# Full-height score matmuls against a zero-padded q, padded by SBUF-to-SBUF DMAs, in a kernel of sparse attention and a two-layer network

## The chip, the cores and the metric

The kernel runs on one core of a Trainium2 chip. The metric is the device time of one execution in microseconds (us), median of several; lower is better. A run comes with the clock granted to TensorE, as a share of full speed. PE is TensorE's matmuls, PEld its weight loads, DVE is VectorE, ACT is ScalarE, POOL is GpSimd, SP is SyncE (which only issues transfers here); SPq and POOLq are their queues of issues. A transfer *lands* when its data have arrived and a waiting engine may go on. A *stop* or *hole* is a time in which TensorE stands still. A *drain* is the time that TensorE takes to empty itself when the number of rows in use changes. PSUM is the memory that TensorE writes its results to. Each run has a state: *slow* if its time is over 1.5% above the fastest of the same kernel, else *fast*.

## The reference

```python
# attention: batch 8, 8 heads, 576 positions, head size 64
scores = scale * (q @ k^T)
local   = (rel >= 0) & (rel < 32)                       # heads 0 to 3
strided = (rel >= 0) & (pos_k % 32 == pos_q % 32)       # heads 4 to 7
out = softmax(masked scores) @ v
# network on the 4608 tokens: 512 -> 2048 -> 512
h = x @ w_in
g = max(h, 0) + alpha * min(h, 0)
y = g @ w_out
```

The inputs q and k are drawn at 0.1 of unit size, so all scores are near zero.

## The kernel before

The network is cut into 9 chunks of 512 tokens; pieces of attention are woven between the pieces of its two layers, so that TensorE always has a dense matmul to do. Heads go in pairs: `g = 4*batch + pair`, pairs 0 and 1 local, 2 and 3 strided. q and k of a pair stand transposed on 128 partitions, one head (or, for strided pairs from batch 3 on, one of two positions) on rows 0 to 63, the other on rows 64 to 127. A score group multiplies each half on its own:

```python
# score_piece: groups of 3 tiles of 96 queries (local) or 4 tiles of 72 (strided)
for x, t in enumerate(grp):
    ...
    for y in range(2):
        hf = slice(64 * y, 64 * y + 64)
        matmul(sps[y][:, w*x : w*x + w], P.kT[hf, k0 : k0 + 128],
               P.qT[hf, q0 : q0 + w], ...)          # 64 rows, two halves side by side
```

From batch 3 on (`DX = 3`) the strided q and k are transposed by DMA, not by TensorE:

```python
def load_d(b):            # GpSimd: q, k of batch b, heads 4..7 -> qks
def transpose_d():        # SyncE: qks -> qT1, kT1 by DMA transpose, q first
```

What is issued where, in the weave of pair g (c is its batch; cuts marked by ...):

```python
okT = 8 <= t < npair and (t % 4 == 0 or t < 4*DX and t % 2 == 0)     # t = g + 1: local transposes
seq: S (scores 0), P (PV 0), T (transpose q), X, S2 (scores 1), P, Tk (transpose k), P
todo = casts of v                       if g % 4 == 0
todo = casts of the next local q and k, each followed by the load of the one after   if g % 4 == 1
...
if lastp:                                # after the last P of the pair
    if g % 4 == 0 and DX <= c < B: transpose_d()
    if g % 4 == 2 and DX <= c and c + 1 < B: load_d(c + 1)
    if g % 4 == 2 and c + 2 < B:             load_v(c + 2, False)
```

The softmax here doesn't subtract the row's maximum and nothing guards it: scores larger than these inputs give would overflow.

Of the kernel before, what the change touches and what calls it, by code (L numbers as in the profile page):

```python
# [10 lines left out]
F16 = mybir.dt.float16  # L11
# [20 lines left out]
def kernel(  # L32
# [10 lines left out]
    nc = tc.nc  # L43
    keep = tc.keep_in_program_order

    B, H, S, D = q.shape
# [7 lines left out]
    cpool = ctx.enter_context(tc.tile_pool(name="const", bufs=1))  # L54
# [15 lines left out]
            name=nc.get_next_instruction_name(), act_func_set_id=6, ins=[], outs=[]  # L70
# [8 lines left out]
    mfirst, mother, mstr = consts[:, 128:416], consts[:, 224:320], consts[0:72, 416:488]  # L79
# [7 lines left out]
    DX = 3  # L87
    qTs = [cpool.tile([128, 2, 672], F16, name=f"qT{i}") for i in range(2)]
# [2 lines left out]
    vss = [cpool.tile([128, 4, 8, 65], F16, name=f"vs{i}") for i in range(2)]  # L91
    ets = [cpool.tile([128, 640], F16, name=f"et{i}") for i in range(NE)]
    x16s = cpool.tile([80, 1024], F16)
    qks = {nm: cpool.tile([80, 4, 512], F16, name=f"{nm}sd") for nm in "qk"}


# [27 lines left out]
    def transpose_d():  # L124

        for nm, dst in (("q", qTs[1]), ("k", kTs[1])):
            o = dst.rearrange("r e c -> r (e c)")[:, 0:1280].rearrange("r (j p) -> r j p", p=80)
            keep(nc.sync.dma_start_transpose(o, qks[nm].rearrange("p h c -> p (h c)")))

    def cast_s(b, nm, eng):  # L130
        t16 = hpool.tile([128, 2, 512], F16, tag=f"{nm}s", bufs=3, name=f"{nm}s")
# [8 lines left out]
    def load_tail(b, strided):  # L140

        t16 = tpool.tile([128, 512], F16, tag="tl", name="tl16")
        for i, src in enumerate((q, k)):
            if strided:
                keep(nc.gpsimd.dma_start(
                    t16[32 * i : 32 * i + 32, :].rearrange("x (h c) -> x h c", h=4),
                    src[b, 4:8, 512:576, :].rearrange("h (x c) d -> x h (c d)", c=2)))
            else:
                keep(nc.gpsimd.dma_start(
                    t16[64 * i : 64 * i + 64, 0:256].rearrange("p (h d) -> p h d", h=4),  # L150
                    src[b, 0:4, 512:576, :].rearrange("h p d -> p h d")))
        cast16[(b, strided, "tail")] = t16
# [122 lines left out]
    def score_piece(P, i):  # L275

        et = ets[ectr["i"] % NE]
        if wide["on"] and ectr["i"] % 2:
            sps = [phpool.tile([128, 512], F32, tag="hps", name="sph") for _ in range(2)]
        else:  # L280
            sp = pbpool.tile([128, 2, 512], F32, tag="sp", name="sp")
            sps = [sp[:, y] for y in range(2)]
        ectr["i"] += 1
        w, grp = P.w, P.sgroups[i]
        n = w * len(grp)
        r = 72 if P.strided else 128
        early = P.b < NEARLY
        for x, t in enumerate(grp):
            if P.dx:
                q0 = k0 = 80 * (4 * (2 * P.pr + t % 2) + t // 2)  # L290
            else:
                q0, k0 = w * t, 32 + 72 * t if P.strided else 96 * t
            for y in range(2):
                hf = slice(64 * y, 64 * y + 64)
                keep(nc.tensor.matmul(  # L295
                    sps[y][:, w * x : w * x + w], P.kT[hf, k0 : k0 + 128],
                    P.qT[hf, q0 : q0 + w], start=(x == 0),
                    stop=(x == len(grp) - 1 and not early), skip_group_check=True))

                key = (2 * (t // 2) + y, t % 2) if P.strided else (t, y)  # L300
                P.et[key] = (et, n * y + w * x)
        first = not P.strided and i == 0
        if early:

            if first:
                m = madd[:, 0:288]
            else:
                m = madd[0:72, 288:360] if P.strided else madd[:, 96:192]
                m = m.unsqueeze(1).to_broadcast([r, n // w, w])
            for y in range(2):  # L310
                keep(nc.tensor.matmul(  # L311
                    sps[y][:, 0:n], ident[0:r, :], m, start=False, stop=True, skip_group_check=True))
        ev = et[0:r, 0 : 2 * n]
        if wide["on"] and ectr["i"] % 2 == 0:
            for y in range(2):
                keep(nc.scalar.activation(
                    ev[:, n * y : n * y + n], sps[y][0:r, 0:n], AF.Exp, scale=SCALE))
        else:
            keep(nc.scalar.activation(  # L319
                ev.rearrange("r (y c) -> r y c", y=2), sp[0:r, :, 0:n], AF.Exp, scale=SCALE))  # L320
        if early:
            return
        if first:
            ev = ev.rearrange("r (y c) -> r y c", y=2)
            m = mfirst.unsqueeze(1).to_broadcast([r, 2, n])
        else:
            ev = ev.rearrange("r (c f) -> r c f", f=w)
            m = (mstr if P.strided else mother).unsqueeze(1).to_broadcast([r, 2 * n // w, w])
        keep(nc.gpsimd.tensor_tensor(ev, ev, m, op=ALU.mult))  # L329
# [57 lines left out]
    npair = 4 * B  # L387
# [61 lines left out]
    for g in range(7, npair + 2):  # L449
        c = g // 4  # L450
        a, p, t = g, g - 1, g + 1
        okA = 8 <= a < npair
        okP = 8 <= p < npair
        okT = 8 <= t < npair and (t % 4 == 0 or t < 4 * DX and t % 2 == 0)
        nP = len(pairs[p].pgroups) if okP else 0
        seq = []
        if okA:
            seq.append(("S", Sc(a, 0)))
        if okP:
            seq.append(("P", Pv(p, 0)))  # L460
        if okT:
            seq.append(("T", T(t // 2, "q")))
        if 8 <= g - 2 < npair and not pairs[g - 2].xd:
            seq.append(("X", X(g - 2)))
        if okA:
            seq.append(("S2", Sc(a, 1)))
        if okP:
            seq.append(("P", Pv(p, 1)))
        if okT:
            seq.append(("Tk", T(t // 2, "k")))  # L470
        if nP == 3:
            seq.append(("P", Pv(p, 2)))
        if not seq:
            seq.append(("N", lambda: None))

        todo = [(c, pr) for pr in range(2)] if g % 4 == 0 and 8 <= g < npair else []

        if g % 4 == 1 and 9 <= g and c + 1 < B:
            todo = [(c + 1, nm) for nm in "qk"]
        lastP = max([i for i, z in enumerate(seq) if z[0] == "P"], default=len(seq) - 1)  # L480
        copyP = next((i for i, z in enumerate(seq) if z[0] == "S2"), 0)
        nslots = [i for i, z in enumerate(seq) if z[0][0] != "S"] or list(range(len(seq)))
        for i, (kind, fn) in enumerate(seq):
            extra = []
            if todo and i in nslots:
                left = len([z for z in nslots if z >= i])
                cnt = -(-len(todo) // max(1, left))
                extra = [todo.pop(0) for _ in range(min(cnt, len(todo)))]

            def run(fn=fn, extra=extra, g=g, c=c, kind=kind, lastp=(i == lastP), copyp=(i == copyP)):  # L490
                fn()
                for b, pr in extra:
                    if pr in ("q", "k"):
                        cast_l(b, pr)
                        if b + 1 < B:
                            load_qk(b + 1, False, pr)
                        continue
                    cast_v(b, pr, "pool")
                    if pr == 1 and b + 1 < B:
                        load_v(b + 1, True)  # L500
                if kind == "Tk" and g % 4 == 3 and c + 3 < B:
                    load_tail(c + 3, False)
                if lastp:
                    if 4 * DX <= g - 1 < npair and pairs[g - 1].xd:
                        x_dma(pairs[g - 1])
                    if g % 4 == 0 and DX <= c < B:
                        transpose_d()
                    if g % 4 == 2 and DX <= c and c + 1 < B:
                        load_d(c + 1)
                    if g % 4 == 2 and c + 2 < B:  # L510
                        load_v(c + 2, False)
                if copyp and 4 * DX <= g - 2 < npair and pairs[g - 2].xd and pairs[g - 2].strided:
                    x_copy(pairs[g - 2])
            feed(run, g - 2 if kind == "X" else -1)
# [98 lines left out]
    def load_unit(b, strided, v_too=True):  # L613
        load_qk(b, strided, "q")
        load_qk(b, strided, "k")
        load_tail(b, strided)
        if v_too:
            load_v(b, strided)
# [83 lines left out]
    while pos["i"] < end1:  # L702
        attn_step(end1)
    wide["on"] = False
    load_unit(3, False)
    load_d(3)

# [48 lines left out]
```

## Time and profile before

| what | before |
|---|---|
| median, range | 334.2 us, 334.1 to 334.5 |
| span in the profile | 332.4 us |
| PE, DVE, ACT, POOL busy | 96%, 56%, 52%, 43% |
| granted clock | 1.00 |

The prediction shows the page and timeline lines. One line more of the kernel before, from the table of stretches: stretch, its length, then busy us of PE, PEld, DVE, ACT and POOL (with counts), granted clock, DMA share and GB/s.

```profile
118.00:152.00 34.00, 33.61 (x268) 16.14 (x266) 19.69 (x39) 19.42 (x32) 18.96 (x18) 1.00 1.03 135
```

In the 34 us of one batch TensorE is busy 33.6 us at full clock. Where costs are worked out below, one dense matmul of 512 columns counts 0.2157 us from start to start, as in the prediction (0.216 is the median of the trace).

### The profile page before, as it was taken

How to read it: one execution, taken by the hardware profiler on the slowest of the kernel's cores; microseconds unless marked ns; L12 is line 12 of the kernel's file. 1: busy time of each engine (PE TensorE's matmuls, PEld its weight loads, DVE VectorE, ACT ScalarE, POOL GpSimd, SP SyncE). 2: the span in 40 equal slices, each digit the busy share in tenths (PEclk: the TensorE clock that was granted, in tenths of full speed). 3: DMA queues.
4: the chain of work that ended last, by engine and by line, in shares of the span. 5: the costliest groups of instructions: out<-in, count | busy, mean ns of one | idle time of the engine just before them, and what ended most of it. 6: DMA issues, size and time to landing. Idle time of an engine off the chain costs nothing.

```text
span 332.4 us, 6351 instructions
## 1 busy us (share of the span) xinstructions
PE 320.5 (96%) x2533; PEld 163.2 (49%) x2533; DVE 185.1 (56%) x363; ACT 172.5 (52%) x300; POOL 142.2 (43%) x154
## 2 busy tenths in 40 slices
PE   6899999999999999999999999999999999999995
PEld 2554455554554444444558754445444444444444
DVE  5477836477553873387428833784368337605800
ACT  2644753467535744575457644773476336425611
POOL 7932497137679365736483528332611400000000
PEclk9999999999999999999999999999999999999999
DMA  6999999399398649683979295715530120011011
GB/s 220 191 207 207 236 210 194 85 245 157 66 87 125 200 59 147 114 234 40 154 138 221 25 153 109 133 13 109 129 67 20 49 85 33 0 65 63 0 63 65
DMA packets 73117, 39.22 MB, mean 118 GB/s; under 512 B 54064, under 2 KB 64768, under 8 KB 73088
## 3 DMA queue, kind: packets, MB, share of 16 engines
q0 software_dynamic: 41760, 17.38, 48.7%
q1 hardware_dynamic: 31328, 21.44, 26.0%
q8 instruction: 20, 0.33, 0.4%
q14 instruction: 9, 0.07, 0.1%
HBM read 38.01 MB, written 9.44 MB: 143 GB/s over the span
## 4 chain that ended last, share of the span: by engine, by line
PE 89%; DVE 4%; ACT 3%; DMA 2%; issue 1%; SPq 0%; ACTq 0%
PE ops L586 37%; PE hps L544 36%; PE pv L345 4%; PE sp L295 4%; PE tp L235 3%; DMA ql<-in_q_dram 2%; DVE x L354 1%; PE wps L608 1%; PE ops L577 1%; ACT xT L366 1%; DVE qT L177 1%; ACT osb L591 1%; PE sp L311 1%; PE sph L311 1%; PE xp L362 1%
## 5 line engine op out<-in xcount | busy, mean ns | idle before, releaser
L586 PE MATMUL ops<-wout,gT 128*128 128x512 f16 x560 | 136.9, 379 | 0.2 <-DVE gT L557 0.2
L544 PE MATMUL hps<-xT,win 128*128 128x512 f16 (+1 forms) x640 | 134.3, 358 | 2.5 <-ACT xT L366 2.0
L557 DVE SCALAR_TENSOR_TENSOR gT<-neg,oma,hps 128x512 f16<-128x512 f32 x144 | 106.0, 744 | 49.8 <-ACT neg L554 42.2
L554 ACT ACTIVATE neg<-hps 128x512 f32<-128x512 f32 x144 | 86.0, 597 | 46.4 <-PE hps L544 45.2
L329 POOL TENSOR_TENSOR et<-et,consts 128x576 f16<-128x576 f16 (+1 forms) x48 | 61.1, 1274 | 95.4 <-ACT et L319 95.3
L544 PEld LDWEIGHTS <-win 128*128 128x128 f16 x640 | 59.4, 98 | 59.4 <-issue 6.1
L586 PEld LDWEIGHTS <-gT 128*128 128x128 f16 x560 | 48.3, 97 | 46.3 <-issue 0.5
L319 ACT ACTIVATE et<-sp 72x576 f16<-72x576 f32 (+1 forms) x56 | 36.1, 645 | 29.2 <-PE sp L295 15.3
L591 ACT COPY osb<-ops 128x512 f32<-128x512 f32 x35 | 20.5, 585 | 53.4 <-PE ops L586 49.6
L352 DVE RECIPROCAL rc<-pv 72x6 f32<-72x6 f32 (+2 forms) x80 | 14.9, 186 | 55.7 <-PE pv L345 55.6
L354 DVE TENSOR_TENSOR x<-pv,rc 96x384 f16<-96x384 f32 (+2 forms) x65 | 34.5, 531 | 2.2
L345 PEld LDWEIGHTS <-et 72*128 72x128 f16 (+1 forms) x448 | 23.4, 98 | 16.5 <-DVE x L354 1.1
L295 PEld LDWEIGHTS <-kT 64*128 64x128 f16 x448 | 10.8, 95 | 26.5 <-issue 21.2
L295 PE MATMUL sp<-qT,kT 64*128 64x72 f16 (+1 forms) x392 | 16.9, 201 | 1.9 <-ACT kT L175 1.7
L177 DVE COPY qT<-tp 128x1024 f16<-128x1024 f16 (+1 forms) x11 | 11.3, 1030 | 12.3 <-PE tp L235 12.3
L608 PE MATMUL wps<-wrm 128*128 128x512 f16 x44 | 15.7, 428 | 1.2 <-DVE wrm L620 1.2
L167 POOL DMA_DIRECT2D vl<-in_v_dram x8 | 11.1, 1394 | 10.7 <-PE xp L362 9.1
L345 PE MATMUL pv<-vs,et 72*128 72x65 f16 x256 | 15.3, 194 | 0.1
L179 POOL COPY vs<-stv 72x1024 f16<-72x1024 f16 x14 | 14.3, 1032 | 0.0
L175 ACT COPY kT<-tp 128x1024 f16<-128x1024 f16 (+1 forms) x11 | 9.4, 858 | 8.4 <-PE tp L235 8.4
L345 PE MATMUL pv<-vl,et 128*128 128x65 f16 x192 | 11.1, 194 | 0.0
L383 ACT COPY xT<-xs 128x576 f16<-128x576 f16 x5 | 6.5, 1301 | 5.2 <-DMA xs<-x16s 5.2
(73 smaller groups left out, 169.5 us busy)
## 6 DMA issues: line engine op xcount, KB each, us to landing
out_dram<-osb SPq DMA_DIRECT2D x35, 256.0 KB, 2.3
ql<-in_q_dram SPq DMA_DIRECT2D x6, 512.0 KB, 5.5
kl<-in_k_dram SPq DMA_DIRECT2D x6, 512.0 KB, 6.6
stv<-in_v_dram POOLq DMA_DIRECT2D x8, 288.0 KB, 6.2
vl<-in_v_dram POOLq DMA_DIRECT2D x6, 384.0 KB, 9.8
win<-in_moe_w_in_dram POOLq DMA_DIRECT2D x4, 512.0 KB, 10.1
wout<-in_moe_w_out_dram POOLq DMA_DIRECT2D x4, 512.0 KB, 17.1
ql<-in_q_dram POOLq DMA_DIRECT2D x3, 512.0 KB, 8.9
```

The costliest lines, as they stand in the source:

```text
L295: keep(nc.tensor.matmul(sps[y][:, w * x : w * x + w], P.kT[hf, k0 : k0 + 128], P.qT[hf, q0 : q0 + w], start=(x == 0), stop=(x == len(grp) ...
L319: keep(nc.scalar.activation(ev.rearrange("r (y c) -> r y c", y=2), sp[0:r, :, 0:n], AF.Exp, scale=SCALE))
L329: keep(nc.gpsimd.tensor_tensor(ev, ev, m, op=ALU.mult))
L345: keep(nc.tensor.matmul(pv[:, 65 * x : 65 * x + 65], et[0:r, c : c + 128], v16[0:r, 2 * P.pr + hh, t, :] if P.strided else v16[:, 6 * (2 * ...
L352: keep(nc.vector.reciprocal(rc[0:w, 0:nb], pvv[:, :, 64]))
L354: keep(nc.vector.tensor_tensor(P.x16[0:w, c0 : c0 + 64 * nb].rearrange("r (c e) -> r c e", e=64), pvv[:, :, 0:64], rc[0:w, 0:nb].unsqueeze ...
L544: keep(nc.tensor.matmul(hps[:, dst : dst + w], win16[:, kk, 128 * m : 128 * m + 128], xT[:, kk, src : src + w], start=(kk == 0 and x == 0) ...
L554: keep(nc.scalar.activation(neg, hps, AF.Relu, scale=-1.0))
L557: keep(nc.vector.scalar_tensor_tensor(gTs[n][:, m, :], neg, oma[:, m : m + 1], hps, op0=ALU.mult, op1=ALU.add))
L586: keep(nc.tensor.matmul(ops, gTs[n][:, kf, 128 * mt : 128 * mt + 128], wout16[:, kf, :], start=(kf == 0), stop=(kf == 15)))
L591: keep(nc.scalar.copy(osb, ops))
L608: keep(nc.tensor.matmul(wps, wrm[:, 0:128], wrm, start=True, stop=True))
```

## The change

The intent: each tile's two halves become one full-height matmul. A padded copy `qz` holds two blocks of q for each tile, the first with rows 64 to 127 zero, the second with rows 0 to 63 zero. One block of keys (128 rows) then serves a moving operand of `2w` columns. TensorE streams twice the columns, but the 64-row mode is left. The padded copies are made by DMA from `qT`; their zeros are written once, by GpSimd before batch 3. To give the copies time, the local transposes go one pair earlier (with the small loads that follow them), and the casts and loads of q and k change places with the casts of v and the load of the strided v that follows them.

```diff
+    qzs = [cpool.tile([128, 2, 1280 if i else 1152], F16, name=f"qz{i}") for i in range(2)]
+    mloc = cpool.tile([128, 576], F16)
...
+    def pad_q(u):                                  # two DMAs of 64 partitions on SyncE
+        src = qTs[u % 2].rearrange("r e c -> r (e c)") if u % 2 else qTs[0][:, :, 0:576]
+        for y in range(2):
+            hf = slice(64 * y, 64 * y + 64)
+            if u % 2:
+                keep(nc.sync.dma_start(qzs[1][hf, y, :], src[hf, 0:1280]))
+            else:
+                keep(nc.sync.dma_start(
+                    qzs[0][hf, y, :].rearrange("r (e c) -> r e c", e=2), src[hf]))
...
+            if P.b >= DX:
...
+                qz = qzs[1 if P.strided else 0]
+                c = 2 * w * x
+                cuts = [(0, 2)] if c // n == (c + 2 * w - 1) // n else [(0, 1), (1, 2)]
+                for y0, y1 in cuts:
+                    bk, o = divmod(c + w * y0, n)
+                    keep(nc.tensor.matmul(
+                        sps[bk][:, o : o + w * (y1 - y0)], P.kT[:, k0 : k0 + 128],
+                        qz[:, y0:y1, q0 : q0 + w], ...))
...
-        okT = 8 <= t < npair and (t % 4 == 0 or t < 4 * DX and t % 2 == 0)
+        okT = 8 <= t < 4 * DX and t % 2 == 0
+        if 4 * DX <= g + 2 < npair and g % 4 == 2:
+            okT, t = True, g + 2
...
-        todo = [(c, pr) for pr in range(2)] if g % 4 == 0 and 8 <= g < npair else []
-        if g % 4 == 1 and 9 <= g and c + 1 < B:
+        todo = [(c, pr) for pr in range(2)] if g % 4 == 1 and 8 <= g < npair else []
+        if g % 4 == 0 and 8 <= g and c + 1 < B:
             todo = [(c + 1, nm) for nm in "qk"]
...
+                if kind == "Tk" and t >= 4 * DX:
+                    pad_q(t // 2)
...
                     if g % 4 == 0 and DX <= c < B:
                         transpose_d()
+                        pad_q(1)
```

## The prediction

> **What bounds the kernel now.** I read the page's busy table and slices first, then the table of stretches, the PE timeline of one batch, and last the DMA issues around the point where the change puts a new transfer.
>
> The busy table and the two slice rows of the kernel before:
>
> ```profile
> PE 320.5 (96%) x2533; PEld 163.2 (49%) x2533; DVE 185.1 (56%) x363; ACT 172.5 (52%) x300; POOL 142.2 (43%) x154
> ...
> PE   6899999999999999999999999999999999999995
> ...
> PEclk9999999999999999999999999999999999999999
> ```
>
> TensorE is busy from end to end at the full granted clock and nobody else passes 56%. So what counts is TensorE time: work on it, or waits of it. Busy time alone hides short stalls (matmul records overlap), so I read start times. The PE timeline of one batch that the change touches (start, length of the merged group, operation, count):
>
> ```profile
> 203.37 1.03 PE L586 MATMUL ops<-wout,gT 128*128 128x512 f16 x4
> 204.33 0.30 PE L295 MATMUL sp<-qT,kT 64*128 64x96 f16 x6
> 204.56 1.04 PE L586 MATMUL ops<-wout,gT 128*128 128x512 f16 x4
> 205.44 0.35 PE L345 MATMUL pv<-vl,et 128*128 128x65 f16 x6
> 205.62 1.03 PE L586 MATMUL ops<-wout,gT 128*128 128x512 f16 x4
> 206.48 0.42 PE L362 MATMUL xp<-consts,x 72*128 72x72 f16 x8
> 206.74 0.81 PE L544 MATMUL hps<-xT,win 128*128 128x512 f16 x3
> 207.91 2.10 PE L544 MATMUL hps<-xT,win 128*128 128x512 f16 x9 [0.35 <-ACT xT L366]
> ...
> 212.09 1.89 PE L544 MATMUL hps<-xT,win 128*128 128x512 f16 x8
> 213.92 0.30 PE L295 MATMUL sp<-qT,kT 64*128 64x72 f16 x8
> 214.15 1.90 PE L544 MATMUL hps<-xT,win 128*128 128x512 f16 x8
> ```
>
> Four dense matmuls of 512 columns take 206.48 - 205.62 = 0.86 us start to start, 0.2155 each: 512 columns at 0.417 ns plus some 2.5 ns. Eight transposes of 72 columns take 0.26 us and six PV matmuls of 65 take 0.18: the same rate, with no loss when they begin or end. The score groups (L295, 64 rows) alone lose time: four dense from 203.37 should have handed over at 204.23, and the score starts at 204.33, **0.10 us later**; and after it another hole before 204.56.
>
> **What the Trainium skill says.** "TensorEngine Tiling (Array Packing)", Key Properties: "Changing tiling mode (not just tile) drains the TensorE". The trace agrees in its sign and gives the size: some 0.1 us going into a 64-row group and the like coming out, and none between groups of 72, 96 and 128 rows, which are evidently one mode. "TensorE: Matmul & The Clock Gate", Back-to-back issue gap, gives N/2.4 + 2.5 ns warm; the 0.2155 us above agrees (213.3 + 2.5 = 215.8). The same page's row on small-K matmuls says that two 64-row halves run concurrently; the change gives that up. "DMA: Bandwidth & Descriptors", anatomy of one DMA, gives about 2 us fixed per transfer (stated for the GpSimd path) and says that a wait is held by the issuing sequencer; here a 256 KB store from SyncE lands in 2.3 us (DMA issues on the page).
>
> **The change, part by part.**
>
> *Score matmuls.* Per batch there are 4 pairs of 2 score groups. Batches 3 to 7 make 40 groups, 20 local and 20 strided. Now, cost of a group = start of the dense run after it minus start of the dense run before it minus the dense matmuls:
> local 204.56 - 203.37 - 4 x 0.2157 = 0.327 us; strided 214.15 - 212.09 - 8 x 0.2157 = 0.334 us.
> After: each tile's two halves become one moving operand of 2w columns against one full-height block of keys. A local group of 3 tiles has 6 x 96 = 576 columns; its middle tile crosses the bank edge and is cut in two, so 4 matmuls. A strided group has 4 matmuls of 144, also 576 columns. Both: 576/2.4 + 4 x 2.5 = 0.250 us. The array streams **twice** the columns, but without the two drains. Saving 20 x 0.077 + 20 x 0.084 = **3.2 us**, 1.0% of the run. All of it lies on TensorE, the bound, so it should show in full. The count of score matmuls falls from 280 to 160 in these batches, all matmuls from 2533 to 2413 or so. Weight loads are at most 128 columns, some 98 ns each but hidden (PV does one each 30 ns), so they stay hidden.
>
> *Masks and exp.* Same 576 columns; the masks read a stored 128x576 pattern instead of a broadcast for the first local group. Zero in effect: 1.27 us each on POOL, which has slack.
>
> *Setup.* Four memsets and six small copies on POOL, queued after the casts that end near 56 us, where POOL then idles 9.1 us until 65.2 and again 7.3 us before 76.6. A 32-column memset took 0.33 us; even some 2.5 us for each of the long ones (my estimate by size, generous) would fit. Zero.
>
> *Order.* The local transposes move one pair earlier (same batch), the casts of q and k change places with those of v. The same pieces are in each chunk. The wait of 0.5 us at 207.91 (ACT copies xT after the output copy) is of a part that does not move; I expect it to stay.
>
> *The pads.* Per batch four SBUF-to-SBUF transfers of 64 partitions, 147 or 164 KB each, 0.6 MB a batch, some 18 GB/s beside the 102 to 135 GB/s in the table of stretches. Volume is harmless. **Latency is the question**: for the strided pairs the pad can be issued only after the DMA transpose of q has landed, and the scores then wait for pad, not transpose. DMA issues of batch 4 (135 us on), median us to landing:
>
> ```profile
> stv<-in_v_dram POOLq DMA_DIRECT2D x1, 288.0 KB, 6.0
> qT<-qsd SPq DMA_TRANSPOSE x1, 7.5
> kT<-ksd SPq DMA_TRANSPOSE x1, 7.2
> ```
>
> and SyncE's and PE's timelines there:
>
> ```profile
> 135.72 1.34 SPq L128 DMA_TRANSPOSE qT<-qsd  x1
> 137.15 4.35 SPq L128 DMA_TRANSPOSE kT<-ksd  x1
> ...
> 145.76 0.30 PE L295 MATMUL sp<-qT,kT 64*128 64x72 f16 x8
> ```
>
> q is there at 135.7 + 7.5 = 143.2, k at 144.35, the strided scores at 145.76: a margin of 2.5 us for q. Two pads need two issues of 0.33 us (as a store's) and 2.3 us to land: about 2.9 us. So 0.4 us short here. By the same subtraction for the other batches (issue of the transpose, its landing, start of the strided scores): batch 3 100.7 + 5.9 against 111.7, margin 5.1; batch 5 169.3 + 6.5 against 179.8, 3.9; batch 6 203.4 + 7.4 against 213.9, 3.0; batch 7 237.5 + 3.8 against 250.8, 9.4. Two things move these: in batches 3 to 5 the 1 MB of loads of the next q and k, now issued after the transposes, come **ahead** of them, with the second on SyncE right before (some 0.6 us of issue, and its bytes in front); and the 288 KB load of v, which today runs beside the transposes, comes a step later. Batch 7, which has neither, shows the transpose alone at 3.8 us. I take these two as about even, up to 2 us worse in batches 3 to 5 and better in batch 6. That gives a stall of 1 to 2 us in batch 4, up to 1 in batch 5, none in 3, 6, 7.
> The local pads come from engine transposes issued a whole pair ahead (that is what the earlier order buys), over 7 us before use: at the edge when they share the queues with the v loads (a transpose of x issued there took 7.6 us), so I allow some tenths.
>
> Sum: -3.2 (scores) + about 1.0 (waits for pads) = -2.2 us: 334.2 - 2.2 = **332.0 us**.
>
> **The rivals.** (a) *Pads fully hidden*: 331.0 us. For: the transpose lands early if v's load no longer competes. (b) *The pad becomes the new wait*: SyncE holds its queue until q has landed and the strided scores of each batch stop TensorE by 1 to 3 us, 3 to 10 us in all: 333 to 341. For: margins of 2.5 to 3.9 us against a need of 2.9. Against: only three batches have the loads in front. (c) *Doubled columns cost more than thought*, with a two-part moving operand read slower or full-height weights not loaded ahead: at 90 ns a matmul a group costs 0.36 us and the change loses 1 us. Against: PV and transposes, full height with weights of their own each, run at column rate. (d) *SyncE held back delays the output stores* until the 3 output buffers run out. Against: the last store of a chunk falls there, and the next is some 9 us off, so no stall.
>
> **Range and chances.** (a) is the low end, 330.4 with some tenths for waits that vanish as well; (b) in its middle is the high end, 335.5. Faster by over 2% needs under 327.6, twice the whole gain: 0.02. Slower by over 2% needs 341, all of (b): 0.03. Within: 0.95.
>
> **What would show it.** The score groups at L313 should have 128 rows, 160 of them, and take 0.25 us between dense runs without the 0.1 us holes. TensorE's wait lists should show a pad landing, if at all, before the first strided scores of batches 4 and 5. PEclk must stay at 9. I am wrong if the holes stay at full height, if the matmuls of 144 and 192 columns run slower than their columns, or if the strided scores wait over 2 us for a pad in several batches.

## The result, and the profile after

The changed kernel takes **359.1 us** (355.9 to 359.8) against 334.2. Its ratio to before is 1.072, with a 95% interval of 1.067 to 1.078. Ratios here are the mean time of one kernel's fast runs over that of the other's fast runs of the same rounds, so they are not quite the ratio of the medians. The profiled run is one of 355.9 us.

The page of the kernel after, busy table and two slice rows:

```profile
PE 323.9 (91%) x2413; PEld 171.1 (48%) x2413; DVE 184.5 (52%) x363; ACT 173.6 (49%) x300; POOL 148.3 (42%) x164
...
PE   7899999999999967989597995999899998999995
...
PEclk9999999999999996999989998999999999999999
```

The matmuls fell from 2533 to 2413 as intended, but the PE row now has gaps in the middle, and the clock row has a 6 and some 8s where it had only 9s. The same stretch as shown of before, in the kernel after:

```profile
118.00:152.00 34.00, 28.50 (x200) 14.62 (x197) 13.45 (x30) 15.29 (x25) 17.74 (x17) 0.90 0.99 141
```

TensorE is busy 5 us less here, and at a mean clock of 0.90. Its timeline in that stretch (start, length of the merged group, operation, form, count, idle time before it and what ended it):

```profile
122.27 1.89 PE L622 MATMUL ops<-wout,gT 128*128 128x512 f16 x8
123.99 0.41 PE L313 MATMUL sp<-qz,kT 128*128 128x144 f16 x4
124.24 1.03 PE L622 MATMUL ops<-wout,gT 128*128 128x512 f16 x4
...
128.44 1.03 PE L622 MATMUL ops<-wout,gT 128*128 128x512 f16 x4
134.62 0.64 PE L313 MATMUL sp<-qz,kT 128*128 128x192 f16 x4 [5.15 <-DMA qz<-qT]
135.05 1.91 PE L622 MATMUL ops<-wout,gT 128*128 128x512 f16 x4
```

Three things stand here. The strided group at 123.99 costs 124.24 - 122.27 - 8 x 0.2157 = 0.244 us, as predicted and less than the 0.334 of before. The local group should have begun at 128.44 + 4 x 0.2157 = 129.30, but TensorE stood still until 134.62 for `qz`. And the four dense matmuls behind that stop show 1.91 us, where four show 1.03 otherwise: they run at half clock (the table of stretches gives 0.50 for 131.6 to 138.4 us). The waits by cause have one row for TensorE's own waits for the pads (total us, times, longest):

```profile
PE sp L313 <- DMA qz<-qT: 17.8, 6, 5.1
```

By start times, the six holes are 5.3, 4.1, 4.2 and 1.5 us before local scores (batches 4 to 7) and 1.5 and 2.3 us before strided ones (batches 4 and 5): 18.9 us. The run's loss is 355.9 - 334.2 = 21.7 us, and 3.2 were to be gained, so some 6 us more are lost. About 5 of them (1.8, 1.7 and 1.5) are columns at half clock behind the three longest stops: the time from the end of the stop to the next group at full rate, less what the same work takes at full rate. The last 1 us is not traced. Why the pad is late is in the DMA issues around it (size, us from issue to landing; rows of other transfers cut):

```profile
vl<-in_v_dram POOLq DMA_DIRECT2D x1, 384.0 KB, 13.2
qsd<-in_q_dram POOLq DMA_DIRECT2D x1, 288.0 KB, 5.5
ksd<-in_k_dram POOLq DMA_DIRECT2D x1, 288.0 KB, 7.3
qz<-qT SPq DMA_DIRECT2D x2, 144.0 KB, 9.4
...
xT<-x SPq DMA_TRANSPOSE x1, 8.0
```

The two local pads, issued at 123.4 and 124.1 us, land after 8.5 and 10.4 us (9.4 is the median). Loads of 0.96 MB went out at 121 to 123 us.

### The profile page after: what moved, and what is told of

Same layout as the page of the kernel before. It is cut to its first block, busy times and chain, and to the rows that moved or that the text cites. A ratio compares the mean times of both kernels' runs of the same rounds, so it can differ in the third digit from the quotient of the medians.

```text
span 354.1 us, 6157 instructions
## 1 busy us (share of the span) xinstructions
PE 323.9 (91%) x2413; PEld 171.1 (48%) x2413; DVE 184.5 (52%) x363; ACT 173.6 (49%) x300; POOL 148.3 (42%) x164
## 4 chain that ended last, share of the span: by engine, by line
PE 67%; DMA 17%; DVE 6%; ACT 4%; SPq 2%; issue 1%; POOL 1%; ACTq 0%
PE hps L580 29%; PE ops L622 24%; DMA qz<-qT 13%; DMA qT<-qsd 3%; PE pv L376 3%; PE sp L313 2%; DVE gT L593 2%; DVE x L385 2%; PE tp L248 2%; DMA ql<-in_q_dram 1%; PE wps L644 1%; DVE qT L190 1%; PE sp L324 1%; PE ops L613 1%; ACT neg L590 1%
## 5 line engine op out<-in xcount | busy, mean ns | idle before, releaser
L622 PE MATMUL ops<-wout,gT 128*128 128x512 f16 x560 | 140.9, 388 | 0.2 <-DVE gT L593 0.2
L580 PEld LDWEIGHTS <-win 128*128 128x128 f16 x640 | 60.3, 98 | 59.7 <-issue 6.8
L360 POOL TENSOR_TENSOR et<-et,consts 72x576 f16<-72x576 f16 (+1 forms) x38 | 48.4, 1275 | 83.8 <-ACT et L348 83.6
L622 PEld LDWEIGHTS <-gT 128*128 128x128 f16 x560 | 50.6, 99 | 46.3 <-issue 3.4
L313 PE MATMUL sp<-qz,kT 128*128 128x144 f16 (+2 forms) x160 | 17.0, 230 | 17.9 <-DMA qz<-qT 17.8
L313 PEld LDWEIGHTS <-kT 128*128 128x128 f16 x160 | 12.7, 100 | 28.8 <-issue 20.0
L360 POOL TENSOR_TENSOR et<-et,mloc 128x576 f16<-128x576 f16 x10 | 12.7, 1273 | 32.6 <-ACT et L348 32.6
```

Of the source, the lines that this page charges most:

```text
L313: keep(nc.tensor.matmul(sps[bk][:, o : o + w * (y1 - y0)], P.kT[:, k0 : k0 + 128], qz[:, y0:y1, q0 : q0 + w], start=(o == 0), stop=(o + w ...
L360: keep(nc.gpsimd.tensor_tensor(ev, ev, m, op=ALU.mult))
L580: keep(nc.tensor.matmul(hps[:, dst : dst + w], win16[:, kk, 128 * m : 128 * m + 128], xT[:, kk, src : src + w], start=(kk == 0 and x == 0) ...
L622: keep(nc.tensor.matmul(ops, gTs[n][:, kf, 128 * mt : 128 * mt + 128], wout16[:, kf, :], start=(kf == 0), stop=(kf == 15)))
```

## The experiments

All times are medians; before ran 334.1 to 334.2 us. Kernels in which TensorE waits for late transfers scatter by 1 to 9 us; those without such waits repeat within 0.2 us (e5, e8, e12) to 1.2 us (e6), except e9 (below). That a race between transfers and TensorE decides the scatter is likely but not shown. Several experiments build on another: e5 on e3, e6 on e1, e10 on e7, e11 on e10, e8 on e7, e9 on e8.

| run | what | us | ratio to before, 95% |
|---|---|---|---|
| e1_stale_q | changed kernel, pads of batch 3 only | 339.3 | 1.012 to 1.019 |
| e2_pads_unread | the same, later pads into an unread tile | 350.1 (fast runs alone 345.7) | 1.029 to 1.040 |
| e3_order_only | the changed order alone | 343.5 | 1.024 to 1.032 |
| e4_local_only | full height for local pairs alone | 355.9 | 1.063 to 1.070 |
| e5_loads_behind | e3, loads back behind the transposes | 334.8 | 1.000 to 1.003 |
| e6_stale_q_loads_behind | e1, loads back | 332.0 | 0.993 to 0.995 |
| e7_pads_loads_behind | changed kernel, loads back | 354.2 | 1.056 to 1.061 |
| e10_v_load_later | e7, v load moved | 342.9 | 1.026 to 1.029 |
| e11_v_and_d_later | e10, loads of strided q, k moved too | 337.7 | 1.009 to 1.012 |
| e8_dve_and_q_early | local pads by VectorE, strided q early | 337.7 | 1.009 to 1.012 |
| e9_dve_t_back | e8, local transposes back in place | 331.4 | 0.991 to 0.997 |
| e12_local_by_dve | before, local pairs full height by VectorE | 332.9 | 0.995 to 0.997 |

My theory after the result: TensorE stops for pads that land late, and long stops lower the clock (L). The rivals: full-height matmuls bring the clock down by themselves (C), the pads' traffic delays other transfers (T), or the new order is at fault (O).

**e1_stale_q.** Later batches score with the q of batch 3: a wrong result.

```diff
     def pad_q(u):
+        pads[u % 2] += 1
+        if pads[u % 2] > 1:
+            return
```

> The changed kernel with the padding transfers of batch 3 alone; batches 4 to 7 score with the stale q of batch 3, so the result is wrong on purpose, but the matmuls, their operands' kind and the order stay. Theory L (TensorE stops for pads that land late, and the stops lower the clock): 331.0 us, 3.2 below before, within 0.7; clock 1.00; no hole before the score groups. Rival C (full-height score matmuls bring the clock down by themselves): clock below 1 and over 338 us. Rival O (the changed order of transposes, casts and loads): some 355 us still.

Measured 339.3 us (337.4 to 341.8), clock 0.99 to 1.00. C is refuted: the same matmuls ran, and the profiled run had a clock of 1.00. But L missed by 8 us: something besides the pads costs time. In the profiled run two strided groups wait for `kT<-ksd`, the DMA transpose of k, 4.6 us together.

The run also passed the comparison with the reference, although its q is stale: with scores near zero the softmax hardly depends on q. So "correct" is a weak word for this path. I therefore recomputed before, after, e9 and e12 in a functional simulation with q and k 12 times larger: all four agree with the reference within 0.0006 relative, while e6, which has a stale q, is off by 0.67. e7, e8, e10 and e11 agree with the reference too.

**e2_pads_unread.** Pads issued, nobody waits for them (wrong result).

```diff
-                keep(nc.sync.dma_start(qzs[1][hf, y, :], src[hf, 0:1280]))
+                keep(nc.sync.dma_start(to[1][hf, y, :], src[hf, 0:1280]))   # to: an unread tile from batch 4 on
 (local pads alike; and, to make room, twice:)
-            t16 = hpool.tile([128, 2, 512], F16, tag=f"{nm}s", bufs=3, name=f"{nm}s")
+            t16 = hpool.tile([128, 2, 512], F16, tag=f"{nm}s", bufs=2, name=f"{nm}s")
```

> As the run with stale q, but all the padding transfers are issued as in the changed kernel, from batch 4 on into a tile that nobody reads (wrong result on purpose; two early buffers of q and k are one fewer to make room). Theory L: the transfers alone cost little, 331 to 332.5 us. Rival T (the pads' traffic delays other transfers, or their place on SyncE's queue delays stores and x transposes, and TensorE waits for those): 345 us or more.

Measured 343.2 to 352.6 us in four runs, two of which count as slow by their time; the two fast ones are 343.2 and 348.1. So with transfers that nobody reads the run is 4 to 9 us longer than e1: T has a share. The fewer buffers were not tested alone, but up to 95.6 us the traces of e1 and e2 run within 0.1 us of each other. The one profile of e2 is of a run that counts as slow (352.2 us), so its sums say only where TensorE can wait: 8.5 us for k's DMA transpose (4.6 in e1), 5.5 for xT (2.8) and 3.1 for pads of batch 3 (1.0). The size of T, and how it splits between the bytes and the place on SyncE's queue, stay open.

**e3_order_only.** Half-height scores as before, no pads.

```diff
-            if P.b >= DX:
+            if False:
...
     def pad_q(u):
+        return
```

> The changed order of transposes, casts and loads alone: half-height score matmuls as before, no pads. Theory L: 334.2 us as before, within 0.7. Rival O: 345 us or more.

Measured 343.5 us: O has a share of 9 us, which L did not expect. TensorE's timeline of this run, at the strided scores of batch 5:

```profile
180.23 1.91 PE L583 MATMUL hps<-xT,win 128*128 128x256 f16 x16
185.80 0.42 PE L329 MATMUL sp<-qT,kT 64*128 64x72 f16 x8 [3.66 <-DMA kT<-ksd]
186.16 3.60 PE L583 MATMUL hps<-xT,win 128*128 128x256 f16 x16
```

and its DMA issues around it:

```profile
kT<-ksd SPq DMA_TRANSPOSE x1, 10.0
```

k's transpose took 10.0 us to land; in the kernel before it took 6.1 us in the same batch. The scores waited 3.7 us for it, and the 16 matmuls behind the stop took 3.60 us instead of 1.91: half clock again. In this profile the two waits for k make 5.9 us, and 5.6 us at half clock behind the longer one lose some 2.8 more, together about the 9 us.

**e4_local_only.**

```diff
-            if P.b >= DX:
+            if P.b >= DX and not P.strided:
...
     def pad_q(u):
+        if not (u % 2 == 0):
+            return
```

> Full-height score matmuls and pads for the local pairs alone; the strided ones as before. Theory L, from the holes before local scores in the profile of after (0.2 + 5.3 + 4.1 + 4.2 + 1.5 = 15.3 us), some 3 us of half clock behind them and half of the gain (1.6): about 351 us. If the strided pads, which my prediction named, were the larger part: under 342 us.

Measured 355.9 us, 12 more than the order alone: the local pads are the largest single part. Its four stops before local scores are 4.9, 4.6, 3.9 and 1.4 us. The strided part then adds little (359.1 for the whole).

**e5_loads_behind.** Which part of the order?

```diff
 (e3, and:)
-        todo = [(c, pr) for pr in range(2)] if g % 4 == 1 and 8 <= g < npair else []
+        todo = [(c, pr) for pr in range(2)] if g % 4 == 0 and 8 <= g < npair else []
-        if g % 4 == 0 and 8 <= g and c + 1 < B:
+        if g % 4 == 1 and 9 <= g and c + 1 < B:
```

> The run of the order alone (343.5 us), with one part of the order undone: the casts of the next q and k, and the loads that follow them, come behind the DMA transposes again, as before; the local transposes stay one pair earlier; half-height scores, no pads. Theory Q (the 1 MB of loads ahead of the DMA transposes makes the transposed k land late, and the strided scores wait for it): 334.2 us, within 1, and no strided score group waits for k. Rival M (the earlier place of the local transposes is what costs): 341 us or more still.

Measured 334.8 us, and no score group waits for k. The strided scores of batch 5 start without a hole:

```profile
179.77 0.30 PE L329 MATMUL sp<-qT,kT 64*128 64x72 f16 x8
```

So the loads ahead of the transposes are what makes the 9 us of e3; the rest of the order (the earlier local transposes) costs 0.6 us. But this rest takes most of the margin. In this batch k's transpose goes out at 173.15 us and lands at 179.73, 0.04 us before its scores. In the kernel before it goes out at 170.81, for scores at the same 179.77. In e5 SyncE's queue is held longer by an output store ahead of the transposes, which waits for a copy on ScalarE (136.49 against 134.69 us in batch 4). In e3 k goes out about as late, 6.3 us before its scores are due (6.5 and 6.6 in e5, 8.6 and 9.0 in before). What the loads add is the longer way to landing: 8.5 and 10.0 us in batches 4 and 5, against 5.3 and 6.6 in e5.

**e6_stale_q_loads_behind.** e1 with the same two lines.

> The run with stale q (wrong on purpose, 339.3 us) with the loads behind the transposes again. Theory Q: the clean gain of the full-height matmuls shows, 331.0 us (3.2 under before), up to 332 with the pads of batch 3 in it; clock 1.00. If full-height matmuls gain nothing or cost: 334 us or more.

Measured 332.0 us, clock 1.00; the profiled run took 331.15, the other four 332.0 to 332.3. This is the gain without the late transfers: 2.2 us by medians, 3.1 in the profiled run. The pads of batch 3 and the 0.6 us of e5 are in it. Its timeline at a local group:

```profile
201.42 1.03 PE L627 MATMUL ops<-wout,gT 128*128 128x512 f16 x4
202.28 0.41 PE L318 MATMUL sp<-qz,kT 128*128 128x192 f16 x4
202.53 1.03 PE L627 MATMUL ops<-wout,gT 128*128 128x512 f16 x4
```

202.53 - 201.42 - 4 x 0.2157 = 0.247 us, against 0.327 of before.

**e7_pads_loads_behind.** The changed kernel, correct, with the same two lines.

> The changed kernel, correct, with the loads behind the transposes again. If the pads' own late landing is a cause of its own: the local score groups of batches 4 to 6 still stop TensorE for some 4 us each, half clock behind them: 345 to 350 us. If the loads in front were the whole cause: 331 to 333 us.

Measured 354.2 us. With the loads put back the pads still make the run 20 us longer than before: two causes, each enough to undo the gain.

**e10_v_load_later and e11_v_and_d_later.** Why do local pads land late? From e7, loads are moved away from them, first that of the local v, then those of the strided q and k too.

```diff
-                    if g % 4 == 2 and c + 2 < B:
+                    if g % 4 == 2 and c + 2 < B and c < DX - 1:
                         load_v(c + 2, False)
+                    if g % 4 == 1 and DX <= c and c + 1 < B:
+                        load_v(c + 1, False)
 (e11 also:)
-                    if g % 4 == 2 and DX <= c and c + 1 < B:
+                    if g % 4 == 3 and DX <= c and c + 1 < B:
                         load_d(c + 1)
```

> Correct. Pads by DMA and loads behind the transposes (354.2 us), with one more part moved: the local v load (384 KB, 10 to 13 us to land) goes out three quarters of a batch later, away from the local pads. Theory B (the local pads land late because they share the engines with the burst of loads issued just before them): the local pads land in 5 to 6 us instead of 8 to 10, the stops before local scores fall to under 2 us, no half clock: 336 to 343 us. If the pads are slow by themselves or through the transpose of x issued just ahead: 350 us or more.

> Correct. As the run before it, and the two loads of the next strided q and k (288 KB each) also moved, one pair later. Theory B: the local pads land in 3 to 4 us, no stop before local scores: 333 to 338 us, with what the moved loads cost elsewhere. If not the burst: as the run before it.

The DMA issues of the local pads of batch 4 (median of the two, us to landing), in e10:

```profile
qz<-qT SPq DMA_DIRECT2D x2, 144.0 KB, 7.8
```

and in e11:

```profile
qz<-qT SPq DMA_DIRECT2D x2, 144.0 KB, 2.9
```

The same transfer takes 9.4 us beside three loads (in e7 as in the changed kernel), 7.8 beside two and **2.9 beside none**. The times follow: 354.2, 342.9, 337.7 us. In e10 the landing fell less than I expected (5 to 6), but the longest stop still halved, from 5.1 to 2.5 us. The transpose of x still goes out 1.3 us before these pads in e11, so it is not what holds them up. In e11 no local group waits any more; what remains is two waits for strided pads, 2.1 us together, and longer waits for xT, 5.5 us against 2.0 before.

**e8_dve_and_q_early.** (From e7.) The pads cross no partitions, so VectorE can write the two halves straight from the transposes' PSUM tile. And the DMA transpose of the strided q can go out one pair before that of k, so that its pads need not wait for it.

```diff
+        if nm == "q" and b >= DX:
+            for y in range(2):
+                hf = slice(64 * y, 64 * y + 64)
+                z = qzs[0][hf, y, :].rearrange("r (e c) -> r e c", e=2)[:, :, 0:512]
+                cast_copy("dve", z.rearrange("r e (p t) -> r e p t", t=8), main[hf])
+            return
 (tails alike)
...
-                        transpose_d()
+                        transpose_d("k")
                         pad_q(1)
+                    if g % 4 == 3 and DX <= c + 1 < B:
+                        transpose_d("q")
```

> Correct. As the last run, but the local padded copies are written by VectorE straight from the transposes' PSUM tile (two halves of 64 partitions for one of 128, so some 1.4 us more VectorE work a batch), and the DMA transpose of the strided q goes out one pair ahead of that of k, so that its pads are issued beside k's transpose. Theory: no score group waits over 0.5 us, 331 to 332 us. If the remaining strided pads still land late in the traffic: stops of 1 to 3 us before strided groups, 334 to 340 us.

Measured 337.7 us (337.5 to 337.7, so hardly any scatter). No score group waits for a pad; the expected time was still missed by 6 us, through a wait I had not named. The timeline of all engines (cut to two rows):

```profile
116.86 2.46 DVE L189 COPY qz<-tp 64x1024 f16<-64x1024 f16 x2
...
120.15 1.89 PE L591 MATMUL hps<-xT,win 128*128 128x512 f16 x8 [1.35 <-DVE gT L604]
```

VectorE's two copies hold it for 2.5 us in the first layer, where it has 0.74 us of work for each 0.86 us of TensorE's. The `gT` results behind them come late, TensorE waits for them (presumably for the PSUM tiles that they free) and stops 1.4 us, in four batches, 5.4 us in all.

**e9_dve_t_back.** The local transposes return to their old place, in the second layer, where VectorE has slack.

```diff
-        okT = 8 <= t < 4 * DX and t % 2 == 0
-        if 4 * DX <= g + 2 < npair and g % 4 == 2:
-            okT, t = True, g + 2
+        okT = 8 <= t < npair and (t % 4 == 0 or t < 4 * DX and t % 2 == 0)
```

> Correct. The last correct run (337.7 us; VectorE writes the local halves, q's DMA transpose early) with the local transposes back one pair later, where before has them, so that VectorE's two copies of 1.2 us fall into the second linear layer, where it has slack, instead of the first, where its share is 0.74 of each 0.86 us. Theory: the four waits of 1.4 us for gT vanish and nothing takes their place: 331.0 to 331.8 us. If the strided pads then land late again (they come up to 1.5 us earlier in the queue of work): 332.5 to 335.

Measured **331.4 us** (ratio 0.9935, 0.991 to 0.997): some 0.6% below before, clear of noise. The four waits for `gT` are gone, as expected. Its timeline in batch 4:

```profile
128.36 1.03 PE L631 MATMUL ops<-wout,gT 128*128 128x512 f16 x4
129.22 0.41 PE L324 MATMUL sp<-qz,kT 128*128 128x192 f16 x4
129.47 1.03 PE L631 MATMUL ops<-wout,gT 128*128 128x512 f16 x4
```

The group starts when the dense matmuls end and costs 1.11 - 0.863 = 0.247 us. Four of six runs lie at 330.9 to 331.9, one at 332.7 and one at 334.7. In the profiled run the strided pads of batch 4 land at 144.5 us, 7.0 to 8.0 us after their issue, and their scores start at 144.8, so I suppose, but have not shown, that the scatter is this thin margin.

**e12_local_by_dve.** Before, with the local pairs alone at full height, by VectorE; no pads by DMA.

> Correct. Before, with full-height scores for the local pairs alone, their padded q written by VectorE from PSUM, everything else in the order of before, no DMA pads. Theory: half the gain, 334.2 - 1.6 = 332.6 us within 0.4, clock 1.00, no wait for gT beyond that of before.

Measured 332.9 us (332.8 to 333.0): half the gain, without scatter.

## Why the prediction was wrong

- **The cost of the scores: right.** Predicted 0.250 us a group, measured 0.244 and 0.247; the drains are gone. e6 shows the gain without the late transfers, 2.2 us by medians (3.1 in its fastest run) against 3.2. The two 64-row halves of before did run side by side, which full height gives up: in the trace they start 4 ns apart. (The page's row that the prediction names speaks of slices of 32 rows.)
- **The order: wrong.** The step "The same pieces are in each chunk" counted TensorE's pieces and found nothing. For the strided pads it did say that 1 MB of loads came ahead of the transposes, but it worked out the margin of q alone (2.5 us in batch 4). k lands later and its margin was in the lines I showed: 145.76 - 144.35 = 1.4 us. It also allowed "some 0.6 us of issue" for the new order, but in e3 k's transpose goes out 6.3 us before its scores are due in batches 4 and 5, against 8.6 and 9.0 in the kernel before. e3 and e5 show that k's lateness costs 9 us, with no pad in the program. The supposed relief by the v load is also not seen in batches 4 and 5: k's transpose took 8.5 and 10.0 us in e3, against 7.2 and 6.1.
- **The local pads: wrong, and the largest part.** The prediction gave them "over 7 us before use" and "some tenths". They had 129.3 - 123.4 = 5.9 us, and needed 8.5 to 10.4. I had quoted that a transpose of x issued there took 7.6 us, and yet allowed only some tenths; by that figure and the true window the second pad would have come over 2 us late. So the step that failed is this wait: TensorE waits 15.1 us for local pads, in four batches. e10 and e11 show that the loads issued just before are the cause: 9.4, 7.8, 2.9 us.
- **The strided pads: right in batch 4 by luck, too small in batch 5.** Predicted 1 to 2 us in batch 4 and up to 1 in batch 5; measured 1.5 and 2.3. In batch 4 q landed 3.5 us before the scores were due, not 2.5 or less, and the two pads needed 4.9 us, not 2.9; in batch 5 they needed 6.2.
- **Rival (b) came nearest, but it was bounded at 10 us.** It named only strided pads, which made 3.8 of the 18.9 us, and it left out what a long stop does to the clock: the stops of 3.9 us and more in the profile after are followed by matmuls at half rate, which loses some 5 us in all.
- **Rivals (c) and (d)** did not occur: the groups of 576 columns took 0.244 to 0.247 us, and TensorE has no wait for an output buffer in its list of waits.
- The prediction's own tests of being wrong named the right symptom, "the strided scores wait over 2 us for a pad in several batches", but at the wrong pairs: strided scores waited over 2 us in one batch, local ones in three.

## What to carry to other kernels

A new transfer is costed at the place where it will be issued: take the landing time of a neighbour in that very stretch, and subtract it from the time to first use, for each of its consumers and for every transfer that the new order pushes back. When the bound engine's gain is 1%, one late landing per batch costs more than the change can give. Where data stay on their partitions, let an engine with slack in that stage write them, and check its slack in that stage and not over the span.

## What the Trainium skill lacked or had wrong

- "TensorEngine Tiling (Array Packing)", Key Properties, says that a mode change drains but not what it costs. Here a drain of some 0.1 us each way made a 64-row group (6 or 8 short matmuls) cost 0.33 us, and the same group at full height, with twice the columns, 0.245. The page recommends row tiling for a contraction of 64 or less without a word on short runs between full-height matmuls.
- "DMA: Bandwidth & Descriptors", anatomy of one DMA, gives about 2 us fixed and a rate per byte (a fit for transfers that GpSimd issues), with no figure for a transfer issued behind others. A pad of 144 KB, issued by SyncE, landed in 2.9 us in a quiet stretch (e11) and in 9.4 behind three loads; the DMA transpose of q took 3.8 us in batch 7 of before, with no new loads beside it, and that of k up to 10.0 (e3).
- "TensorE: Matmul & The Clock Gate", the table under "Why this matters for your kernels", warns of idle gaps over some 3 us. The runs agree for long stops: behind 3.66 us (e3) and 5.15 us (after) the matmuls ran at half rate, for 5.6 and 3.8 us. But they give no sharp limit: behind 3.27 us (e7) and 2.54 us (e10) four dense matmuls still showed 1.03 us, while behind another stop of 2.54 us, in the profile of e2, eight showed 3.33 instead of 1.89.
